# Two edits to a linear attention with two MLPs: where hosted heads make their x, and when the first layer's split weights are stored

## The chip, the core and the metric

The kernel runs on one core of a Trainium2 chip. The metric is device time in microseconds (us) of one execution, lower is better; the kernel before takes 1578.41 us, the median of 3 runs (1578.3 to 1580.91).

## What is computed

Eight batches of eight heads of 576 tokens with 64 columns go through a linear attention with an RMS norm; the heads side by side make 4608 rows of 512 columns, which go through two MLPs (512 to 2048 to 512) in float32.

```
kv  = einsum('bhsd,bhse->bhde', k, v)
out = einsum('bhsd,bhde->bhse', q, kv)
x   = out / sqrt(mean(out*out, -1) + 1e-6) * g_norm        # heads joined: [4608, 512]
h   = x @ w_in
g   = where(h >= 1, h, where(h <= -1, 0, (h + 1)**2 / 4))
x1  = g @ w_out
h2  = x1 @ w_in2
out = relu(h2)**2 @ w_out2
```

The weights arrive as 64-bit numbers; the kernel narrows them itself.

## The kernel before, in words

Every float32 matrix product is made of three TensorE products: both operands are split into a high part and a low rest, and hi x hi, hi x lo and lo x hi are summed in PSUM (`mm3`, L234; in the later phases L858). One such group of three stands in the listings as a row with `x3`.

The columns are taken in blocks of 512 tokens, one block `b` for each batch. **Blocks 0 to 4 of the first MLP are plain** (`PLAIN = 5`). A block has NF = 16 steps `f`. Step `f` computes twelve matmuls into `ph_b_f` (`h_stage`), ACT and DVE make of it `u_b_f` (L682 and L220 on ACT, then L684 on DVE, which frees the PSUM bank of `ph`; two such banks rotate), a split into hi and lo makes `gs_b_f` (L213 on ACT, L226 on DVE), and twelve matmuls add `gs_b_f` times the second weight to four PSUM banks `acc_b` (`out_stage`, two steps later). The first weight `w_0_f` and the second `w_1_f` are loaded as `raw`, narrowed (L264 on ACT, L266 and L267 on DVE as `d`) and split (L182) once, in block 0. All `w_0_f` and `w_1_0` to `w_1_6` stay in SBUF; `w_1_7` to `w_1_15` go to DRAM at once and come back in each later block as tail weights `wt_7` to `wt_15` through three buffers (`load_tail`, L294, SP's queue). Beside that, blocks 1 to 4 prepare the second MLP's weights and sums of both MLPs' weights for the later phases (`prep_...`: raw loads on SP, narrowing L266/L267, sums L334 to L358, splits L182, stores `wsd<-s` issued by ACT, L174).

**The later phases work on pairs of blocks** with seven products in place of eight (`in_phase`, `out_phase`, L858). They read their weights `ws` from the DRAM tiles `wsd`. So the split weights of the first MLP have to be in `wsd` too: `keep_first` stores the parts that the sums don't make, 23 stores (16 of `w_0_f`, 512 KB each for f below 8 and 256 KB above; 7 of `w_1_f`, 256 KB each) on SP's queue. A table of half steps decides when the program writes them: `hook(s, ...)` means step s // 2, first or second half.

**Attention** is done a pair of heads at a time, `hp` = 0 to 3 in a block. `kv_stage` makes k^T v in a PSUM tile `pkv` (L478), ACT copies it into two block-diagonal tiles `kvbd` (L213). `t_stage` transposes q to `qT` on DVE (L548). `o_stage` multiplies (`po`, L557) and ACT makes of each half the square twice (L566 into `s`, L567 into `wk`) and, times the gain, `o` (L205); DVE makes the low rest `s2lo` (L572). `r_stage` sums the squares (`pr`, L586), ACT makes the reciprocal root y (L587) and its square `t` (L220), DVE multiplies o by y (L592), makes a Newton step (`newton`, L516, two halves) and `norm` (L519), the last product that gives x. `pkv`, `po` and `pr` share two PSUM banks (`at`), so each of them waits until the one before the last has been read. The tile `o` is `work[1]`, tag `wk1`, one buffer; `t` in the hosted case is a tile of tag `q`, two buffers that it shares with the loads of q.

The attention of block b is done within block b - 1. That of batches 5 to 7 is **hosted** in the paired phases n = 0 and 1 (`HOSTED`, six pairs of heads each), and there `r_stage` stores x to DRAM (`xpd`, 256 KB, and the last 64 columns `xrd`, 32 KB), on SP's queue.

The order on each engine is static: a scheduler places all instructions by its own estimate of the data's readiness, and the chip then runs each engine's list in order. DMA issues stand in the lists of SP and ACT.

Of the kernel before, what the change touches and what calls it, by code (L numbers as in the profile page):

```python
# [70 lines left out]
def linear_attention_rms_two_mlps(  # L71
# [12 lines left out]
    nc = tc.nc  # L84
# [7 lines left out]
    TB = 512  # L92
# [41 lines left out]
    xpd = {b: dr.tile([P, KD, TB], F32, name=f"xpd{b}") for b in range(PLAIN, B)}  # L134
    x1d = [dr.tile([P, KD, TB], F32, name=f"x1d{b}") for b in range(NB)]
    xrd = dr.tile([P, KD, B, REM], F32, name="xrd")
# [63 lines left out]
    def engine(op, phase):  # L200
        return engines[next(turns[op][min(phase, 2)])]
# [16 lines left out]
    def square(e, dst, src):  # L218
        if e is nc.scalar:
            e.activation(dst, src, AF.Square)  # L220
        else:
            e.tensor_tensor(dst, src, src, ALU.mult)

    def split(t, src, op, phase):
        hi = copy(engine(op + "_hi", phase), t[:, 0, :], src)
        lo = engine(op + "_lo", phase).tensor_tensor(  # L226
            t[:, 1, :], src, t[:, 0, :].bitcast(F32), ALU.subtract
        )
        return hi, lo
# [159 lines left out]
    def bank(b, name):  # L389

        pool, tag = next(banks) if b == 0 else (ps_t, "at")
        return pool.tile([P, TB], F32, tag=tag, name=name)
# [122 lines left out]
    def newton(t, m):  # L515
        nc.vector.scalar_tensor_tensor(t, m, 1e-6, t, op0=ALU.add, op1=ALU.mult)  # L516

    def norm(dst, t, o):
        nc.vector.scalar_tensor_tensor(dst, t, -3.0, o, op0=ALU.add, op1=ALU.mult)  # L519
# [54 lines left out]
    def r_stage(b, hp):  # L574
        (y, o), _ = hl.pop((b, hp))
        if (b, hp) in WHOLE:
            products = [(ones.bitcast(F32), y)]
        else:
            products = [(ones, s2) for s2 in og.pop((b, hp))]
        ms = []  # L580
        for half in range(2):
            c = slice(half * U, (half + 1) * U)
            ps = bank(b, f"pr_{b}_{hp}_{half}")
            m = ps[:, :U]
            for n, (one, s2) in enumerate(products):
                nc.tensor.matmul(m, one, s2[:, c], start=n == 0, stop=n == len(products) - 1)  # L586
            nc.scalar.activation(y[:, c], m, AF.Abs_reciprocal_sqrt, bias=epsb)  # L587
            ms.append((c, m))
        pool, tag = (ap1, "wk2") if b < PLAIN else (ap2, "q")
        t = pool.tile([P, S], F32, tag=tag, name=f"t_{b}_{hp}")  # L590
        square(engine("y", b), t, y)
        nc.vector.tensor_tensor(o, o, y, ALU.mult)  # L592
        for c, m in ms:
            newton(t[:, c], m)
        if b < PLAIN:
            norm(t, t, o)
            nc.gpsimd.tensor_copy(xrem[b][:, hp, :], t[:, TB:])
            split(xs[1, b][hp], t[:, :TB], "x", b)
            return
        norm(o, t, o)  # L600
        nc.sync.dma_start(xpd[b][:, hp, :], o[:, :TB])
        nc.sync.dma_start(xrd[:, hp, b, :], o[:, TB:])

    def new_x(L, b):
        xs[L, b] = [
# [23 lines left out]
    def attention(base, every, order):  # L629

        slots = []
        for j, (b, hp) in enumerate(order):
            s = base + int(every * j)
            turn.setdefault((b, hp), len(turn))
            if b == 1:
                slots += [(max(0, s - 7), load_kv, b, hp), (s, kv_stage, (b, hp))]
            elif j % 2 == 0:
                two = order[j : j + 2]
                turn.setdefault(two[-1], len(turn))
                slots += [(max(0, s - 7), load_kv, *i) for i in two]  # L640
                slots.append((s - (1 if j else 0) - (b < PLAIN and j > 0), kv_stage, *two))
            slots += [
                (max(0, s - (7 if b < PLAIN or j < 2 else 5)), load_q, b, hp),
                (s, t_stage, b, hp),
                (s + 4, o_stage, b, hp, 0),
                (s + 5, o_stage, b, hp, 1),
            ]
            late = 8 if b < PLAIN else 7
            if j == 0 and b < PLAIN:
                slots.append((s + late, begin, b))  # L650
            slots.append((s + late, r_stage, b, hp))
        if b < PLAIN:
            slots.append((2 * NF * b + 2, store_xrem, b))
        return slots
# [426 lines left out]
    def hook(s, f, *a):  # L1081
        hooks.setdefault((s // 2, s % 2), []).append((f, a))
# [17 lines left out]
    last = 2 * (PLAIN - 1) * NF  # L1100
    kept = [(w, f) for f in range(NF) for w in range(2) if w == 0 or f < NF - TAIL]
    for j, (w, f) in enumerate(kept):
        hook(14 + 2 * j, keep_first, w, f)

    units = (
# [201 lines left out]
```

## Time and profile before

| | |
|---|---|
| median of 3 runs | 1578.41 us (1578.3 to 1580.91) |
| profiled execution | 1577.31 us |
| its span in the profile | 1575.5 us |
| granted TensorE clock, mean | 0.993 |
| PE busy | 1544.7 us, 98% of the span |
| DVE, ACT busy | 74%, 57% |
| moved by DMA | 388.14 MB, mean 246 GB/s |

The page gives busy time for each engine, the span in 40 slices and the chain that ended last; 87% of that chain is PE. PE is the engine to watch: a stretch in which it is not busy, or in which the clock granted to it is under 1.00, is lost time. The windows (busy time of each engine in a stretch) show such stretches, the timeline of PE shows in brackets how long it was idle ahead of an instruction and which engine and line released it, and the timelines of DVE, ACT and SP at that time show what stood ahead of the releaser in its queue.

### The profile page before, as it was taken

Reading aid. Unit: us, or ns where it says so; the run is one execution under the profiler, and the core shown is the slowest. Engines: PE = TensorE matmul, PEld = TensorE weight load, DVE = VectorE, ACT = ScalarE, POOL = GpSimd, SP = SyncE. Lnnn points to the kernel's source line nnn. Section 1 sums busy time; section 2 is a strip of 40 time slices with the busy share of each in tenths; the row PEclk is TensorE's granted clock in tenths of the full one; section 3 lists DMA queues with packets and bytes.
Section 4 is the critical chain, followed back from the end, with each engine's and each line's share of the span. In section 5 each row is a group of like instructions: output and inputs, shape, how many; then the busy total and the mean of one; then the engine's idle time right before and its main releaser. Section 6 shows DMA issues by size and latency. Waiting matters only on the chain.

```text
span 1575.5 us, 22117 instructions
## 1 busy us (share of the span) xinstructions
PE 1544.7 (98%) x7581; PEld 1268.8 (81%) x7581; DVE 1169.7 (74%) x2033; ACT 896.1 (57%) x1693; POOL 10.8 (1%) x30
## 2 busy tenths in 40 slices
PE   9999989999999999998999999999999999999999
PEld 5777768887877788787778888888888888888899
DVE  6975777776789668964789788868884597559666
ACT  5875756666656556734566466546653464446354
POOL 0000000000000000000000000000000000000000
PEclk9999999999999999999999999999999999999999
DMA  9776899897799967789867877776776676977797
GB/s 282 199 231 208 239 338 293 278 288 235 237 341 343 334 200 212 243 226 220 250 187 234 229 240 244 223 218 196 245 233 207 198 242 198 243 243 214 223 391 249
DMA packets 330911, 388.14 MB, mean 246 GB/s; under 512 B 197808, under 2 KB 223408, under 8 KB 330800
## 3 DMA queue, kind: packets, MB, share of 16 engines
q1 hardware_dynamic: 299904, 330.63, 70.1%
q10 hardware_dynamic: 30896, 56.11, 9.8%
q8 instruction: 60, 0.98, 0.2%
q14 instruction: 51, 0.42, 0.1%
HBM read 300.42 MB, written 86.25 MB: 245 GB/s over the span
## 4 chain that ended last, share of the span: by engine, by line
PE 87%; DMA 4%; DVE 4%; ACT 3%; issue 1%; SPq 1%; ACTq 0%; DVEq 0%
PE ph L858 31%; PE po L858 31%; PE acc L234 11%; PE ph L234 10%; PE po L557 2%; DMA wt<-wsd 1%; PE pkv L478 1%; PE pr L586 1%; DMA wsd<-s 1%; DVE s L182 1%; DMA ws<-wsd 1%; DMA v<-in_v_dram 0%; DVE u L684 0%; DMA k<-in_k_dram 0%; DVE x L787 0%
## 5 line engine op out<-in xcount | busy, mean ns | idle before, releaser
L858 PE MATMUL ph<-x,ws 128*128 128x512 f32 (+1 forms) x2352 | 508.7, 377 | 0.5 <-DVE u L684 0.5
L858 PEld LDWEIGHTS ph<-x,ws 128*128 128x128 f32 x2352 | 421.0, 190 | 81.0 <-DVE u L684 0.9
L858 PE MATMUL po<-t,ws 128*128 128x512 f32 x2016 | 462.4, 390 | 0.8 <-DVE t L787 0.8
L858 PEld LDWEIGHTS po<-t,ws 128*128 128x128 f32 x2016 | 377.9, 188 | 80.7 <-DVE t L787 2.2
L787 DVE TENSOR_TENSOR t<-g,t 128x512 fp32r<-128x512 f32 (+1 forms) x336 | 216.3, 649 | 86.4 <-ACT t L213 82.9
L213 ACT CAST t<-g 128x512 fp32r<-128x512 f32 (+1 forms) x336 | 195.5, 590 | 117.7 <-PE po L858 63.3
L234 PE MATMUL ph<-x,w 128*128 128x512 f32 x960 | 241.2, 397 | 8.5 <-DVE u L684 7.4
L234 PEld LDWEIGHTS ph<-x,w 128*128 128x128 f32 x960 | 178.4, 188 | 52.3 <-DVE u L684 10.7
L935 ACT ACTIVATE g<-h 128x512 f32<-128x512 f32 (+1 forms) x120 | 70.6, 589 | 111.8 <-DVE h L924 111.8
L234 PE MATMUL acc<-gs,w 128*128 128x512 f32 x528 | 132.4, 395 | 0.4 <-ACT w L213 0.2
L924 DVE CUSTOM_DVE_ANT_0 h<-ph,e 128x512 f32<-128x512 f32 (+1 forms) x120 | 76.3, 637 | 61.0 <-PE ph L858 56.9
L914 DVE TENSOR_TENSOR e<-ph,e 128x512 f32<-128x512 f32 (+1 forms) x112 | 72.3, 650 | 61.3 <-PE ph L858 56.5
L234 PEld LDWEIGHTS acc<-gs,w 128*128 128x128 f32 x528 | 98.2, 188 | 22.2 <-ACT w L213 0.9
L234 PE MATMUL acc<-gs,wt 128*128 128x512 f32 x432 | 107.6, 398 | 3.9 <-DVE gs L226 2.2
L234 PEld LDWEIGHTS acc<-gs,wt 128*128 128x128 f32 x432 | 82.0, 191 | 22.3 <-DVE gs L226 2.6
L213 ACT CAST gs<-u 128x512 fp32r<-128x512 f32 x80 | 49.7, 622 | 65.0 <-DVE u L684 48.8
L682 ACT ACTIVATE u<-ph,halfb 128x512 f32<-128x512 f32 x80 | 55.2, 690 | 48.0 <-PE ph L234 36.1
L213 ACT CAST x<-xr 128x512 fp32r<-128x512 f32 (+1 forms) x98 | 57.2, 589 | 43.1 <-DVE xr L838 24.3
L226 DVE TENSOR_TENSOR gs<-u,gs 128x512 fp32r<-128x512 f32 x80 | 54.9, 687 | 27.0 <-ACT gs L213 26.5
L684 DVE SCALAR_TENSOR_TENSOR u<-u,ph 128x512 f32<-128x512 f32 x80 | 54.3, 681 | 24.1 <-ACT u L220 24.0
L787 DVE TENSOR_TENSOR x<-xr,x 128x512 fp32r<-128x512 f32 (+1 forms) x98 | 63.1, 648 | 2.6 <-ACT x L213 2.6
L911 ACT COPY e<-ph 128x512 f32<-128x512 f32 (+1 forms) x56 | 30.8, 554 | 56.4 <-PE ph L858 49.5
(127 smaller groups left out, 1547.0 us busy)
## 6 DMA issues: line engine op xcount, KB each, us to landing
ws<-wsd SPq DMA_DIRECT2D x392, 512.0 KB, 4.4
wsd<-s ACTq DMA_DIRECT2D x96, 512.0 KB, 5.5
wt<-wsd SPq DMA_DIRECT2D x36, 512.0 KB, 5.5
raw<-in_moe_w_in_dram SPq DMA_DIRECT2D x32, 512.0 KB, 6.6
raw<-in_moe_w_out_dram SPq DMA_DIRECT2D x32, 512.0 KB, 6.5
xr<-x1d SPq DMA_DIRECT2D x36, 256.0 KB, 5.4
out_dram<-ov SPq DMA_DIRECT2D x142, 64.0 KB, 3.5
wsd<-w SPq DMA_DIRECT2D x17, 512.0 KB, 4.2
```

The source lines that it names most:

```text
L213: return e.copy(dst, src)
L226: lo = engine(op + "_lo", phase).tensor_tensor(t[:, 1, :], src, t[:, 0, :].bitcast(F32), ALU.subtract)
L234: nc.tensor.matmul(dst, wt(a), xt(c), start=first and n == 0, stop=last and n == 2)
L557: nc.tensor.matmul(ps[:, :U], kv, qT[:, c], start=True, stop=True)
L682: nc.scalar.activation(u, ps, AF.Relu, bias=halfb, scale=0.5)
L684: nc.vector.scalar_tensor_tensor(u, u, 1.0, ps, op0=ALU.min, op1=ALU.max)
L787: engine2(op + "_lo").tensor_tensor(t[:, 1, :], src, t[:, 0, :].bitcast(F32), ALU.subtract)
L858: nc.tensor.matmul(ps, wt(a), xt(c), start=first and n == 0 and i == 0, stop=last and n == len(lhs) - 1 and i == 2, skip_group_check=True,)
L911: nc.scalar.copy(e[i, 1], bank)
L914: nc.vector.tensor_tensor(e[i, p], bank, e[i, 1], ALU.add)
L924: nc.vector._custom_dve(TENSOR_ADD_SAT, out=h, in0=bank, in1=add, s0=float("inf"), s1=0.0)
L935: nc.scalar.activation(g, h, AF.Square)
```

## The change

```diff
@@ r_stage, for the hosted heads @@
-        norm(o, t, o)
-        nc.sync.dma_start(xpd[b][:, hp, :], o[:, :TB])
-        nc.sync.dma_start(xrd[:, hp, b, :], o[:, TB:])
+        norm(t, t, o)
+        nc.sync.dma_start(xpd[b][:, hp, :], t[:, :TB])
+        nc.sync.dma_start(xrd[:, hp, b, :], t[:, TB:])
@@ the 23 stores of the first layer's split weights @@
     kept = [(w, f) for f in range(NF) for w in range(2) if w == 0 or f < NF - TAIL]
     for j, (w, f) in enumerate(kept):
-        hook(14 + 2 * j, keep_first, w, f)
+        hook(16 + 2 * j // 3, keep_first, w, f)
```

The first edit makes x in the tile `t` in place of `o` and stores it from there. The second moves the 23 stores from half steps 14, 16, ... 58 (one for each step, from step 7 of block 0 to step 13 of block 1) to half steps 16 to 30, that is (2 * j) // 3, three for every two half steps, all within block 0.

No instruction is added or left out; the order changes. The first edit alters it in the paired phase n = 1, the second at the end of block 0 and in block 1. In names, `ph_1_10` is block 1, step 10; in the hosted stage `ph_6_3` is product 6, tile 3, `h_4_3`, `h_3_3` are what DVE makes of the products, and `po_0_0`, `pr_3_1` carry the pair of heads and the half. `pkv_0` and `pkv_2` are made for two pairs at once.

**Place 1: DVE in block 1.** Before, from the split of a prepared second weight (`s_1_0_1`) to `u` of step 10:

```order
L182 TENSOR_TENSOR s_1_0_1_1984<-d_1_8_1914,s_1_0_1_1984 128x2x256
L357 TENSOR_TENSOR s_2_1_0_1953<-s_2_1_0_1953,d_1_0_1884 128x256
L358 TENSOR_TENSOR s_2_1_0_1954<-d_1_8_1914,s_2_1_0_1953 128x256
L334 TENSOR_TENSOR j_0_2011<-w_1_0_490 128x512
L182 TENSOR_TENSOR s_1_0_2_1987<-s_2_1_0_1953,s_1_0_2_1987 128x2x256
L182 TENSOR_TENSOR s_1_0_3_2008<-s_2_1_0_1954,s_1_0_3_2008 128x2x256
L355 TENSOR_TENSOR s_1_1_0_2040<-j_0_2011 128x256
L548 STREAM_TRANSPOSE qT_3_2116<-q_3_1906 128x576
L684 SCALAR_TENSOR_TENSOR u_1_10_2110<-u_1_10_2110,ph_1_10_2097 128x512
```

Now, around the same `u_1_10`:

```order
L684 SCALAR_TENSOR_TENSOR u_1_9_2068<-u_1_9_2068,ph_1_9_2055 128x512
L548 STREAM_TRANSPOSE qT_2_1911<-q_2_1687 128x576
L226 TENSOR_TENSOR x_2_1_1744<-t_1_1950,x_2_1_1744 128x512
L226 TENSOR_TENSOR gs_1_9_2083<-u_1_9_2068,gs_1_9_2083 128x512
L266 TENSOR_SCALAR d_1_0_1891<-raw_1_0_1701 128x512
L684 SCALAR_TENSOR_TENSOR u_1_10_2114<-u_1_10_2114,ph_1_10_2101 128x512
L267 SCALAR_TENSOR_TENSOR d_1_0_1891<-raw_1_0_1701,d_1_0_1891 128x512
```

`u_1_10` has moved ahead of the narrowing, sums and splits of that weight. Some rows above stands `u_1_8`:

```order
L572 TENSOR_TENSOR s2lo_1_1834<-wk_2_1_1671,s_2_1_1805 128x576
L182 TENSOR_TENSOR s_0_0_2_1867<-s_1_0_0_1861,s_0_0_2_1867 128x2x256
L182 TENSOR_TENSOR s_0_0_3_1887<-s_1_0_0_1862,s_0_0_3_1887 128x2x256
L684 SCALAR_TENSOR_TENSOR u_1_8_2009<-u_1_8_2009,ph_1_8_1996 128x512
L592 TENSOR_TENSOR wk_2_1_1672<-wk_2_1_1672,wk_2_1_1671 128x576
L516 SCALAR_TENSOR_TENSOR t_1_1950<-pr_1_0_1942,t_1_1950 128x288
L516 SCALAR_TENSOR_TENSOR t_1_1950<-pr_1_1_1946,t_1_1950 128x288
L226 TENSOR_TENSOR gs_1_8_2021<-u_1_8_2009,gs_1_8_2021 128x512
```

Before, `s2lo_1` and these two splits stood two steps earlier, ahead of `u_1_6`; now `u_1_8` stands behind them.

**Place 2: PE in block 1.** Before, where pair 0 and 1's `pr` and the `pkv` of pairs 2 and 3 stand:

```order
L586 MATMUL pr_1_0_1935<-s_2_1_1796,ones 128x288
L586 MATMUL pr_1_0_1935<-s2lo_1_1826,ones 128x288
L234 MATMUL acc_1_2_1618<-gs_1_5_1806,w_1_5_676 128x512
L234 MATMUL acc_1_3_1619<-gs_1_5_1806,w_1_5_676 128x512 x2
L234 MATMUL ph_1_8_1990<-x_1_0_760,w_0_8_660 128x512 x3
L234 MATMUL ph_1_8_1990<-x_1_1_761,w_0_8_660 128x512 x3
L478 MATMUL pkv_2_1828<-v_3_1673,k_3_1670 64x64 x8
L478 MATMUL pkv_2_1828<-rest_129 64x64 x2
L234 MATMUL ph_1_8_1990<-x_1_2_762,w_0_8_660 128x512 x3
L234 MATMUL ph_1_8_1990<-x_1_3_763,w_0_8_660 128x512 x2
L586 MATMUL pr_1_1_1939<-s_2_1_1796,ones 128x288
L586 MATMUL pr_1_1_1939<-s2lo_1_1826,ones 128x288
```

Now, with `po_1` in the same piece:

```order
L557 MATMUL po_1_0_1803<-qT_1_1673,kvbd_131 128x288
L557 MATMUL po_1_1_1829<-qT_1_1673,kvbd_131 128x288
L234 MATMUL ph_1_9_2055<-x_1_3_763,w_0_9_730 128x512 x2
L478 MATMUL pkv_2_1836<-v_2_1678,k_2_1675 64x64 x8
L478 MATMUL pkv_2_1836<-rest_128 64x64 x2
L586 MATMUL pr_1_0_1942<-s_2_1_1805,ones 128x288
L586 MATMUL pr_1_0_1942<-s2lo_1_1834,ones 128x288
L478 MATMUL pkv_2_1836<-v_3_1684,k_3_1681 64x64 x8
L478 MATMUL pkv_2_1836<-rest_129 64x64 x2
L586 MATMUL pr_1_1_1946<-s_2_1_1805,ones 128x288
L586 MATMUL pr_1_1_1946<-s2lo_1_1834,ones 128x288
L234 MATMUL ph_1_10_2101<-x_1_0_760,w_0_10_786 128x512 x3
```

Between them ph and acc matmuls stood before; now `po_1`, `pkv_2` and `pr_1` stand together, ahead of `ph_1_10`. Further up `ph_1_2` to `ph_1_5` now stand ahead of `pkv_0` and of the first `acc_1` rows. On ACT, `u_1_8`'s L220 stands behind L566, L567 and L205 of both halves of `po_1`, two casts and two stores of a prepared weight, L587 and the `kvbd` copies. On SP the 23 stores are gone from between the loads of block 1; eight more than before stand ahead of its first k load, and `wt_8` still stands behind `raw_1_4` and `raw_1_12`.

**Place 3: PE and DVE in phase n = 1.** PE before, from the last `pr` of pair 3 to the first matmuls behind `po_0`:

```order
L586 MATMUL pr_3_0_7391<-s_6_3_7282,ones 128x288
L586 MATMUL pr_3_0_7391<-s2lo_3_7311,ones 128x288
L586 MATMUL pr_3_1_7395<-s_6_3_7282,ones 128x288
L586 MATMUL pr_3_1_7395<-s2lo_3_7311,ones 128x288
L858 MATMUL ph_5_2_7260<-x_1_3_0_6495,ws_0_1_3_7210 128x512 x3
L858 MATMUL ph_5_2_7260<-x_1_3_1_6697,ws_0_1_3_7210 128x512 x3
L858 MATMUL ph_5_3_7270<-x_1_3_0_6495,ws_0_1_3_7210 128x512 x3
L858 MATMUL ph_5_3_7270<-x_1_3_1_6697,ws_0_1_3_7210 128x512 x3
L557 MATMUL po_0_0_7468<-qT_0_7360,kvbd_130 128x288
L557 MATMUL po_0_1_7496<-qT_0_7360,kvbd_130 128x288
L858 MATMUL ph_1_4_7370<-x_1_1_0_6338,ws_0_2_1_7241 128x512 x3
```

PE now:

```order
L858 MATMUL ph_6_3_7181<-x_1_4_0_6520,ws_0_1_4_7170 128x512 x3
L858 MATMUL ph_6_3_7181<-x_1_4_1_6720,ws_0_1_4_7170 128x512 x3
L557 MATMUL po_0_0_7468<-qT_0_7360,kvbd_130 128x288
L858 MATMUL ph_5_2_7260<-x_1_3_0_6495,ws_0_1_3_7210 128x512 x3
L858 MATMUL ph_5_2_7260<-x_1_3_1_6697,ws_0_1_3_7210 128x512 x3
L858 MATMUL ph_5_3_7270<-x_1_3_0_6495,ws_0_1_3_7210 128x512 x3
L858 MATMUL ph_5_3_7270<-x_1_3_1_6697,ws_0_1_3_7210 128x512 x3
L557 MATMUL po_0_1_7496<-qT_0_7360,kvbd_130 128x288
L586 MATMUL pr_0_0_7557<-s_7_0_7470,ones 128x288
L586 MATMUL pr_0_1_7561<-s_7_0_7470,ones 128x288
L586 MATMUL pr_0_0_7557<-s2lo_0_7501,ones 128x288
L586 MATMUL pr_0_1_7561<-s2lo_0_7501,ones 128x288
```

DVE now, over the same stretch:

```order
L924 ISA h_4_2_7294<-ph_6_2_7172,e_1_1_7152 128x512
L519 SCALAR_TENSOR_TENSOR t_3_7399<-t_3_7399,wk_6_3_7167 128x576
L924 ISA h_4_3_7303<-ph_6_3_7181,e_1_1_7152 128x512
L548 STREAM_TRANSPOSE qT_0_7360<-q_0_7205 128x576
L924 ISA h_3_2_7346<-ph_5_2_7260,e_1_1_7179 128x512
L924 ISA h_3_3_7355<-ph_5_3_7270,e_1_1_7179 128x512
L941 TENSOR_TENSOR t_1_2_7362<-g_1_2_0_7153 128x512
L942 TENSOR_TENSOR g_1_2_0_7153<-g_1_2_1_7154,g_1_2_0_7153 128x512
L941 TENSOR_TENSOR t_1_3_7365<-g_1_3_0_7163 128x512
L572 TENSOR_TENSOR s2lo_0_7501<-wk_7_0_7358,s_7_0_7470 128x576
```

`pkv_0` and `pr_3` have moved 24 matmuls up, `po_0_0` stands directly behind `ph_6_3`, and the four `pr_0`, which stood 60 matmuls behind `po_0_1`, follow it at once. On DVE `qT_0` (L548) stood behind `h_4_3` before too, but on PE the `pkv`, the `pr` and twelve ph matmuls then lay between `ph_6_3` and `po_0_0`. Later in the same phase `pr_1_1` and `po_2_0` stay where they were, and `pkv_2` and `pr_1_0` move 24 matmuls up.

## Rows read from the trace of the kernel before

**Rows 1.** Windows: window, us, busy us of PE, PEld, DVE, ACT, POOL, clock, DMA share, GB/s.

```profile
100.00:120.00 20.00, 19.77 (x105) 15.91 (x104) 14.74 (x26) 14.96 (x31) 0.24 (x1) 1.00 0.55 212
180.00:200.00 20.00, 16.52 (x90) 12.94 (x88) 14.42 (x26) 13.31 (x29) 0.24 (x1) 0.99 0.86 255
200.00:220.00 20.00, 16.12 (x60) 12.78 (x61) 14.36 (x28) 7.96 (x15) 0.24 (x1) 0.83 0.98 338
720.00:740.00 20.00, 17.50 (x71) 14.05 (x70) 9.94 (x16) 9.04 (x18) 0.00 (x0) 0.91 0.88 197
740.00:760.00 20.00, 19.05 (x119) 15.49 (x118) 14.07 (x22) 10.35 (x24) 0.00 (x0) 1.00 0.88 234
780.00:800.00 20.00, 16.06 (x93) 12.63 (x92) 9.86 (x16) 9.57 (x22) 0.00 (x0) 0.83 0.41 139
```

**Rows 2.** Timeline, PE, block 1: start, us, instruction, count, idle before and releaser.

```profile
202.26 0.80 PE L234 MATMUL ph<-x,w 128*128 128x512 f32 x1 [5.73 <-DVE u L684]
...
210.27 5.75 PE L234 MATMUL acc<-gs,wt 128*128 128x512 f32 x24 [1.62 <-DMA wt<-wsd]
```

**Rows 3.** Timeline, DVE, block 1.

```profile
198.84 1.29 DVE L182 TENSOR_TENSOR s<-s,s 128x512 fp32r<-128x512 f32 x2
...
201.51 0.69 DVE L684 SCALAR_TENSOR_TENSOR u<-u,ph 128x512 f32<-128x512 f32 x1 [0.23 <-ACT u L220]
```

**Rows 4.** Timeline, ACT, block 1 (ACTq: its DMA issues).

```profile
197.90 0.62 ACT L213 CAST s<-s 128x512 fp32r<-128x512 f32 x1 [1.15 <-DVE s L357]
...
199.56 0.97 ACTq L174 DMA_DIRECT2D wsd<-s  x2
200.85 0.63 ACT L220 ACTIVATE u<-u 128x512 f32<-128x512 f32 x1 [1.82 <-DVE s L355]
```

**Rows 5.** Timeline, SP's queue, end of block 0 and block 1.

```profile
144.27 4.41 SPq L159 DMA_DIRECT2D wsd<-w  x4
...
201.30 0.94 SPq L294 DMA_DIRECT2D wt<-wsd  x1
```

**Rows 6.** Timeline, PE, hosted attention.

```profile
724.75 1.66 PE L557 MATMUL po<-qT,kvbd 128*128 128x288 f32 x4 [2.50 <-DVE t L516]
...
746.58 0.69 PE L478 MATMUL pkv<-kv 128*64 128x64 f32 x16
...
749.37 0.40 PE L586 MATMUL pr<-s,ones 128*128 128x288 f32 x1 [0.95 <-ACT kvbd L213]
...
787.86 0.40 PE L586 MATMUL pr<-s,ones 128*128 128x288 f32 x1 [0.90 <-ACT kvbd L213]
...
791.43 1.33 PE L557 MATMUL po<-qT,kvbd 128*128 128x288 f32 x2 [3.04 <-DVE qT L548]
```

**Rows 7.** Timeline, DVE, hosted attention.

```profile
749.20 0.77 DVE L548 STREAM_TRANSPOSE qT<-q 128x576 f32<-128x576 f32 x1
...
751.20 0.82 DVE L516 SCALAR_TENSOR_TENSOR t<-pr,t 128x288 f32<-128x288 f32 x2
...
754.11 0.69 DVE L941 TENSOR_TENSOR t<-g 128x512 f32<-128x512 f32 x1
...
756.05 0.75 DVE L572 TENSOR_TENSOR s2lo<-wk,s 128x576 fp32r<-128x576 f32 x1
```

**Rows 8.** Timeline, ACT, hosted attention.

```profile
717.31 0.50 ACT L205 ACTIVATE wk<-po,gvec 128x288 f32<-128x288 f32 x1
...
718.27 0.53 ACT L205 ACTIVATE wk<-po,gvec 128x288 f32<-128x288 f32 x1
...
748.47 0.86 ACT L213 COPY kvbd<-pkv 64x64 f32<-64x64 f32 x4
749.35 1.10 ACT L587 ACTIVATE wk<-pr,epsb 128x288 f32<-128x288 f32 x2
...
758.29 0.89 ACT L205 ACTIVATE wk<-po,gvec 128x288 f32<-128x288 f32 x2 [1.26 <-DMA xrd<-wk]
```

**Rows 9.** The page's DMA issues: operation, count, KB each, us to landing.

```profile
xpd<-wk SPq DMA_DIRECT2D x12, 256.0 KB, 3.1
```

## The prediction, made before the changed kernel was run

> **What bounds the kernel now.** I read the windows of 20 us first, then the engines' timelines around the poor ones, then the DMA queue. TensorE is what the time is made of: in a sound window it is busy for all of its 20 us at granted clock 1.00, and time is lost only where PE idles or its clock falls. The windows name two such places that the change touches. In block 1 (180 to 220 us) PE is busy for 16.52 and 16.12 of 20 us, and the clock of the second window is 0.83 [rows 1]. In the hosted attention (720 to 800 us) it is busy for 17.50, 19.05 and 16.06 us, at 0.91, 1.00 and 0.83 [rows 1]. A clock that averages 0.83 over 20 us costs up to 0.17 x 20 = 3.4 us, and 0.91 up to 1.8.
>
> Block 1 first. PE waits 5.73 us for the DVE instruction u and 1.62 us for the tail weight wt [rows 2]. That u (L684, step 10) starts on DVE at 201.51, only after two splits of a weight preparation [rows 3], and its ScalarE half (L220, 200.85) stands behind two stores that ACT issues [rows 4]: a queue's order, not work, makes PE wait. The wt transfer was issued at 201.30, when PE had already stopped [rows 5]. Loss there: 5.73 + 1.62 = 7.35 idle, and 0.2 + 3.4 of clock from the two windows: **11.0 us**. In the hosted stage I read four waits: 2.50, 0.95, 0.90 and 3.04 us [rows 6], each for a copy or a DVE step of a head.
>
> **Edit 1 (x over t).** No instruction is added or removed; the store's source changes, so the tile that the store holds is t and not o. What this frees is the next head's L205, which writes o. In the trace just one of the twelve heads waited there, 1.26 us on ACT [rows 8], and PE did not wait for it: worth 0. What it burdens is the next t. Two t or q buffers rotate, a head comes about every 19 us (the pr of one head is at 749.37, that of the next but one at 787.86 [rows 6]), and a store lands 3.1 us after its issue [rows 9]: no wait, 0, with some 15 us of cover. A store that landed three times as late would still be covered. So the direct effect is nothing, and what counts is the order that the scheduler now writes in phase n=1. By the listing in the section on the change:
> - pr_3_1 waits for the four kvbd copies, as now (0.95 [rows 6]); ACT now has L587 and a cast ahead of them, so **+0.4**.
> - po_0_0 stands directly behind the last matmul of ph_6_3, and its qT stands on DVE behind h_4_3, which needs that same matmul. One 128x512 step 0.69 and the transpose 0.77 [rows 7]: **+1.5**, where there was no wait.
> - pr_0 now follows po_0_1 at once. Its s2lo comes on DVE behind h_3_3, L941, L942 and L941, four steps of 0.69 and its own 0.75 [rows 7], 3.5 us from the end of ph_5_3, less some 0.8 that PE has to do: **+2.7**. Before, 60 matmuls lay between.
> - pr_1_1 is 24 matmuls later, which covers the kvbd copies: -0.90. po_2_0 behind it then waits for the chain L587, L592, two L516, L519, transpose: 0.55 + 0.76 + 0.82 + 0.76 + 0.77 = 3.7 [rows 7, 8] (the 128x576 steps at 0.76) in place of 3.04: +0.6. Together **-0.3**.
> Sum +4.3. The clock: five and a half us of idle fall into some 16 us from 742. A lone 0.95 in a window left it at 1.00, 2.50 took it to 0.91, 3.94 to 0.83 [rows 1, 6]. These waits are each under 3, so I take the middle one, **+1.8** (ends 0 and 3.4). Edit 1: **+6.1**, 4.3 to 7.7.
>
> **Edit 2 (the 23 stores).** The same 23 stores of 512 or 256 KB (7.8 MB; 17 of them, 5.5 MB, stood behind block 1's first loads) now leave SP within or just after block 0. There the DMA engines have room: 0.55 busy at 100 to 120 us [rows 1]. SP has eight more stores ahead of block 1's first k. Four took it 4.41 us [rows 5], so k is issued some 9 us later; but PE needs k some 11 us later than before, since the four times twelve matmuls of ph_1_2 to ph_1_5 (2.7 us each) now come ahead of pkv_0. So 0. If a store took SP twice as long, 18 less 11 = 7 us would show, which is the upper bound; PE did not wait for SP's loads there, so no gain is to be had.
> In block 1 the 5.73 goes: u_1_10 now stands ahead of the preparation that it was behind. What is late next is a clump. po_1, pkv_2 and pr_1, which were spread between ph and acc matmuls, now stand in a row between ph_1_9 and ph_1_10, and ph_1_10 needs the bank that u_1_8 frees. u_1_8's L220 stands on ACT behind: two sets of L566, L567, L205 at 0.96 a set (from one L205 to the next [rows 8]), two casts of 0.62, L587 at 0.55, two store issues 0.97, the kvbd copies 0.87; with itself 0.63 and L684 0.69 on DVE that is 6.9 us [rows 3, 4, 8]. PE has 1.84 for two pkv halves and two pr (746.58 to 749.37 without the wait), 0.40 for two more pr [rows 6] and 0.45 for two matmuls: 2.7. Wait **4.2**. ph_1_11 then needs u_1_9, behind L587, L682 and L220 on ACT and L516, gs, L519 on DVE, about 4.2 us against the 2.7 of twelve matmuls: **1.5**. wt_8 stands on SP behind raw_1_4 and raw_1_12, whose buffers are freed only after u_1_10; with about 5 us from issue to use, PE waits 0 to 3.5, and I take **1.7**. The clock lies between 1.00 and the 0.83 of today's 7.35 idle: 0 to 3.4, **1.7**. New loss 9.1 against 11.0: **-1.9**, from -9.5 (only the first 1.5 of it comes) to +3.
>
> **Sum.** The profiled execution took 1577.31; +6.1 - 1.9 = +4.2 gives 1581.5. The median of the runs lies 1.1 above that execution; I go half of it up, to **1582**, own range 1578.5 to 1586. The bound of no change, 0.2%, is 3.2 us, so 1575.2 to 1581.6.
>
> A rule that would alter the clock terms is in the Trainium skill, "TensorE: Matmul & The Clock Gate", section "A second HAM failure mode: psum-queue depth-cycling": a kernel whose PE paused briefly and often between groups, as it went round its PSUM banks, had its clock swing between the two levels. The lone 0.95 at full clock [rows 1, 6] does not show this, but no window here has five such waits together. By that rule both clumps would run at 1.2 GHz for a time, which is the third rival, at 1587; without it the clock terms would be 0 and the sum 3.5 lower, at 1578.
>
> **Rivals.**
> 1. *Faster.* Block 1 gives nearly all back. Place: u_1_10 and u_1_8 on DVE and ACT. If the casts and store issues ahead of u_1_8 are done before po_1 arrives (their inputs do not depend on po_1), PE waits little and the clock stays: 1.5 lost in place of 11.0, -9.5. With hosted waits of 4.3 at full clock: 1577.3 - 5.2 = 1572, some 1573 by the median. It decides from 7.5 us given back. For it: 5.5 MB leave a stretch where the DMA engines were 0.86 to 0.98 busy [rows 1]. Against: the kvbd copies do depend on the clump.
> 2. *No change.* Block 1 gives back 5 (wt_8 in time, clock full) and the hosted stage takes 6.1: 1578.4, by the median 1579.5.
> 3. *Slower still.* Both clumps at the lower clock and wt_8 at its worst: hosted 1.6 more (7.7), block 1 1.7 of clock and 1.8 of wt_8 more, so 1581.5 + 1.6 + 3.5 = 1586.6, by the median 1587. For it: 0.83 in both places already today.
> 4. *The order costs nothing.* The listing holds no times: if PE comes to po_0_0 and pr_0 later than I count, it finds their inputs made, and block 1's clump only takes the place of the 7.35 us of today. Then the changed kernel does what it says and stays at 1578. Against: both hosted inputs depend on the very matmul ahead of the wait.
>
> **How the numbers follow.** Forecast 0.41, rivals 0.22, 0.20, 0.12, 0.05. The forecast's low end lies within 0.2% (0.08 of its 0.41). Faster 0.22; within 0.2%: 0.20 + 0.05 + 0.08 = 0.33; slower 0.33 + 0.12 = 0.45. The range 1572 to 1587 leaves out about half of the first rival and some of the third.
>
> **What would show it.** Right: in the changed profile po_0_0 waits 1.5 for qT and pr_0 2.5 to 3 for s2lo and L205, in the window from 740; the 5.73 for u is gone and shorter waits for kvbd, u and wt stand after po_1, at about 185 to 210. Wrong: windows 180 to 220 at 19 or more of 20, or the hosted windows no worse than now. A wait of L220's t for a store of xpd would make the first edit's 0 wrong; a PE wait for v or k at 145 to 155, the second's.

## The result, and the profile after

The changed kernel takes **1595.01 us**, median of 4 runs (1592.14 to 1596.37), against 1579.66 (1578.30 to 1582.27): ratio **1.0093, 95% interval 1.0072 to 1.0114**, 15 us slower. I had forecast slower, 1582, and a range to 1587; the time lies outside it. The head of the profile's page, of an execution that took 1595.61 us:

```profile
span 1593.7 us, 22135 instructions
PE 1554.4 (98%) x7581; PEld 1271.6 (80%) x7581; DVE 1169.7 (73%) x2033; ACT 897.4 (56%) x1693; POOL 10.7 (1%) x30
```

The span is 18.2 us longer than before: PE is idle for 8.5 of these (39.3 in place of 30.8) and busy for 9.7 more at the same 7581 matmuls. The mean granted clock went from 0.993 to 0.990, which stands for some 4.8 of the 9.7. Both executions can also be timed from one matmul to the same matmul. The changed one is 2.0 us later at its first `ph`. The 400 `ph` and `acc` matmuls that begin with block 1's first take it 6.8 us longer (121.0 against 114.2). The hosted stage takes it 5.2 longer (from the `ph` behind its first `pkv` to the first product of `out_phase`: 717.69 to 818.48, against 707.22 to 802.86), and what follows directly 1.4 longer. The other 2.8 lie in stretches that differ by as much from one kernel of this document to another. The medians lie 15.3 apart, so some 3 us of the 18 belong to the two executions and not to the change.

The windows of the changed kernel, the two stretches of [rows 1] (busy us of PE, PEld, DVE, ACT, POOL, then clock, DMA share, GB/s; the hosted stage now begins some 10 us later):

```profile
180.00:200.00 20.00, 16.02 (x93) 12.02 (x92) 14.76 (x28) 10.59 (x25) 0.24 (x1) 0.87 0.89 277
200.00:220.00 20.00, 14.41 (x54) 10.28 (x53) 14.74 (x29) 13.42 (x27) 0.24 (x1) 0.84 0.81 255
220.00:240.00 20.00, 20.00 (x86) 16.48 (x85) 14.51 (x30) 7.05 (x15) 0.00 (x0) 0.94 0.92 291
240.00:260.00 20.00, 18.62 (x114) 14.68 (x114) 17.93 (x33) 14.93 (x30) 0.64 (x1) 1.00 1.04 322
720.00:740.00 20.00, 15.69 (x68) 12.24 (x67) 9.53 (x15) 10.45 (x23) 0.00 (x0) 1.00 0.91 230
740.00:760.00 20.00, 18.06 (x113) 14.39 (x111) 11.26 (x18) 8.87 (x18) 0.00 (x0) 1.00 0.98 231
760.00:780.00 20.00, 16.70 (x65) 13.27 (x66) 10.11 (x17) 9.09 (x18) 0.00 (x0) 0.91 0.58 158
800.00:820.00 20.00, 16.36 (x61) 13.05 (x60) 9.12 (x14) 7.56 (x14) 0.00 (x0) 0.83 0.50 127
```

Block 1 has lost 3.98 + 5.59 + 1.38 us of idle and, at 0.87, 0.84 and 0.94, some 7 us of clock: 18 us in place of 11. The hosted stage, which was the sure part of the forecast, is next. PE's timeline there:

```profile
728.34 0.40 PE L586 MATMUL pr<-s,ones 128*128 128x288 f32 x1 [1.22 <-ACT wk L205]
729.34 0.40 PE L586 MATMUL pr<-s,ones 128*128 128x288 f32 x1 [0.60 <-ACT wk L205]
...
735.27 1.24 PE L557 MATMUL po<-qT,kvbd 128*128 128x288 f32 x4 [2.50 <-DVE t L516]
...
753.49 0.40 PE L586 MATMUL pr<-s,ones 128*128 128x288 f32 x1 [1.40 <-ACT kvbd L213]
...
760.94 0.75 PE L557 MATMUL po<-qT,kvbd 128*128 128x288 f32 x2 [1.47 <-DVE qT L548]
...
766.64 0.40 PE L586 MATMUL pr<-s,ones 128*128 128x288 f32 x1 [1.58 <-ACT wk L205]
767.82 0.53 PE L586 MATMUL pr<-s2lo,ones 128*128 128x288 f32 x2 [0.79 <-DVE s2lo L572]
...
806.99 1.33 PE L557 MATMUL po<-qT,kvbd 128*128 128x288 f32 x2 [3.64 <-DVE qT L548]
```

The first three waits are those of before (the 2.50 is in [rows 6]; the other two, from the kernel before):

```profile
717.87 0.40 PE L586 MATMUL pr<-s,ones 128*128 128x288 f32 x1 [1.23 <-ACT wk L205]
718.86 0.40 PE L586 MATMUL pr<-s,ones 128*128 128x288 f32 x1 [0.59 <-ACT wk L205]
```

Then come the four that the order was read for: 1.40 for kvbd, 1.47 for qT, 1.58 + 0.79 for pr_0, 3.64 for qT. All eight make 13.2 us; the six of before made 9.2. The clock took no more than before: one window at 0.91 and one at 0.83 in both kernels. In block 1:

```profile
154.39 0.69 PE L478 MATMUL pkv<-v,k 128*64 128x64 f32 x16
...
187.27 1.24 PE L557 MATMUL po<-qT,kvbd 128*128 128x288 f32 x4
...
189.27 0.69 PE L478 MATMUL pkv<-v,k 128*64 128x64 f32 x16 [0.30 <-ACT wk L205]
...
190.26 0.40 PE L586 MATMUL pr<-s,ones 128*128 128x288 f32 x1 [0.19 <-ACT wk L205]
...
192.75 0.69 PE L478 MATMUL pkv<-v,k 128*64 128x64 f32 x16 [1.69 <-DMA v<-in_v_dram]
...
194.50 0.40 PE L586 MATMUL pr<-s,ones 128*128 128x288 f32 x1 [0.95 <-ACT kvbd L213]
...
195.88 6.42 PE L234 MATMUL ph<-x,w 128*128 128x512 f32 x15 [0.85 <-DVE u L684]
...
214.90 0.87 PE L557 MATMUL po<-qT,kvbd 128*128 128x288 f32 x2 [2.05 <-DVE t L516]
218.47 10.23 PE L234 MATMUL acc<-gs,wt 128*128 128x512 f32 x36 [2.71 <-DMA wt<-wsd]
...
241.83 3.47 PE L234 MATMUL ph<-x,w 128*128 128x512 f32 x14 [1.18 <-DVE u L684]
```

The 5.73 of [rows 2] is gone, and eleven smaller waits have come. The clump after po_1 (187.27) waits 0.30, 0.19, 1.69, 0.95 and 0.85. After it 15 matmuls take 6.42 us, nearly twice their time, and then follow 2.05 for the bank of po_3, 2.71 for wt and 1.18 for u, with smaller ones between. pkv_0 stands at 154.39 with no wait ahead of it, though SP had issued its k long before:

```profile
120.07 14.73 SPq L159 DMA_DIRECT2D wsd<-w  x12
134.85 1.20 SPq L418 DMA_DIRECT2D k<-in_k_dram  x1
...
157.65 7.93 SPq L159 DMA_DIRECT2D wsd<-w  x10
...
183.24 0.39 SPq L421 DMA_DIRECT2D v<-in_v_dram  x1
```

k goes out at 134.85, after twelve stores in 14.73 us. In the kernel before it went out only 3.35 us earlier:

```profile
131.50 0.84 SPq L418 DMA_DIRECT2D k<-in_k_dram  x1
```

So pkv_0 is late because PE's list has it late. SP's waits from 155 to 192 us (what was waited for, total us, how many, longest) show two that no listing of names tells (the kernel before has such waits too, 7.5 us for `wsd<-s` ahead of a k, 4.6 for x1d):

```profile
SPq L159 <- DMA x1d<-ev: 14.3, 2, 13.4
SPq L421 <- DMA wsd<-s: 7.5, 1, 7.5
```

The ten stores behind the first loads stood 13.4 us for a transfer that ACT issues (x1d, the result of block 0), and the v of pair 2 stood 7.5 us for one of ACT's `wsd<-s`.

### The profile page after: what moved, and what is told of

It reads as the page before. It is cut to its first block, busy times and chain, and to the rows that moved or that the text cites. A ratio compares the mean times of both kernels' runs of the same rounds, so it can differ in the third digit from the quotient of the medians.

```text
span 1593.7 us, 22135 instructions
## 1 busy us (share of the span) xinstructions
PE 1554.4 (98%) x7581; PEld 1271.6 (80%) x7581; DVE 1169.7 (73%) x2033; ACT 897.4 (56%) x1693; POOL 10.7 (1%) x30
## 4 chain that ended last, share of the span: by engine, by line
PE 85%; DMA 7%; DVE 5%; ACT 2%; issue 1%; SPq 0%; ACTq 0%; DVEq 0%
PE ph L858 31%; PE po L858 30%; PE acc L234 10%; PE ph L234 9%; DMA wsd<-s 2%; DMA wt<-wsd 2%; DMA v<-in_v_dram 1%; PE po L557 1%; PE pkv L478 1%; PE pr L586 1%; DMA ws<-wsd 1%; PE pwarm L1161 0%; DVE t L787 0%; DVE s L182 0%; DMA k<-in_k_dram 0%
## 5 line engine op out<-in xcount | busy, mean ns | idle before, releaser
L787 DVE TENSOR_TENSOR t<-g,t 128x512 fp32r<-128x512 f32 (+1 forms) x336 | 217.1, 652 | 87.6 <-ACT t L213 80.0
L226 DVE TENSOR_TENSOR gs<-u,gs 128x512 fp32r<-128x512 f32 x80 | 55.1, 688 | 24.6 <-ACT gs L213 24.0
L787 DVE TENSOR_TENSOR x<-xr,x 128x512 fp32r<-128x512 f32 (+1 forms) x98 | 63.6, 654 | 2.0 <-ACT x L213 2.0
```

The source lines that it names most:

```text
L226: lo = engine(op + "_lo", phase).tensor_tensor(t[:, 1, :], src, t[:, 0, :].bitcast(F32), ALU.subtract)
L787: engine2(op + "_lo").tensor_tensor(t[:, 1, :], src, t[:, 0, :].bitcast(F32), ALU.subtract)
```

## The experiments

All ratios are against the kernel before, run on the same chip: 1578.9 to 1580.4 in the four sets.

**e1, e2: one edit each.** The first edit alone (`norm(t, t, o)` and the stores from t), and the second alone (`hook(16 + 2 * j // 3, ...)`).

> The first edit alone (x made over t, stores where they were before). My theory: the loss of the hosted stage comes from this edit and is a matter of order: po_0_0 waits 1.5 us for qT, pr_0 some 2.4 for L205 and s2lo, po_2_0 3.6 for qT, with the clock lower once; blocks 0 and 1 as before. Time 5 to 6.5 us over the kernel before, about 1585.5. Rival: the first edit is free and the whole loss comes from the stores in block 1, which shifted the hosted stage against its loads: then 1579.7 here, within 1.5 us.

Measured 1587.79, ratio 1.0049 (1.0031 to 1.0066), +4.9 to +10.4 us. The windows 180 to 220 of this run are as before (16.91 and 15.85 busy, clock 1.00 and 0.83), and its hosted stage has the eight waits of the changed kernel, each within 0.02 us, and takes the same 5.2 us longer. The price is above the 5 to 6.5 us that I had expected.

> The second edit alone (stores in block 0 on SP's queue, x made over o). My theory: block 1 loses 18 us in place of 11, the hosted stage is as before: 7 to 9 us over the kernel before, about 1587.5. Rival (the first edit makes all of it): 1579.7.

Measured 1584.91, ratio 1.0036 (1.0027 to 1.0046), +5.7 us, under my 7 to 9. Its waits in block 1 are those of the changed kernel, within 0.6 us each. The two are separate terms: 0.49% and 0.36% make 0.85% of the 0.93%. Both rivals fall.

**e2 on ACT: the same stores at the same half steps, another queue.** `e` is a new argument of `keep_halves`; `keep_first` passes `nc.scalar`.

```diff
-            nc.sync.dma_start(dst, t[:, hs])
+            e.dma_start(dst, t[:, hs])
```

> The second edit alone, with the 23 stores issued by ACT's queue at the same half steps; the same bytes in block 0. Queue theory: what hurts is that 13 stores stand on SP ahead of block 1's k, v and q, so that its attention comes late and in a clump; with SP free block 1's pkv, po and pr stand apart, the 1.69 for v and the waits of the clump go, and block 1 loses 2 to 6 us in place of 18: 1571 to 1576. Traffic theory: the bytes in block 0 collide with the loads whoever issues them: 1586 to 1589. Third: ACT is held by its store issues and u comes late: block 0 loses some us in the place of block 1, 1580 or more.

Measured 1562.84, ratio **0.9889 (0.9873 to 0.9905)**, 17.5 us faster than the kernel before by the ratio, and under my 1571 to 1576. Its windows of block 1, and the first of the hosted stage:

```profile
180.00:200.00 20.00, 20.00 (x90) 16.49 (x90) 17.42 (x33) 13.38 (x27) 3.65 (x1) 1.00 0.88 281
200.00:220.00 20.00, 20.00 (x91) 16.50 (x90) 15.99 (x31) 13.13 (x27) 0.24 (x1) 1.00 1.05 319
700.00:720.00 20.00, 15.69 (x68) 12.28 (x68) 11.97 (x18) 9.50 (x21) 0.00 (x0) 1.00 0.94 237
```

Block 1 loses nothing, with the DMA engines at 0.88 and 1.05, where the changed kernel had 0.89 and 0.81. So bytes in this stretch are not the cause: the traffic theory falls.

**e3: the stores in blocks 2 and 3, on SP.** `hook(64 + 2 * j, ...)`.

> The 23 stores at half steps 64, 66 to 108 (blocks 2 and 3, one for each step, on SP), x made over o. Queue theory: block 1 is rid of them as in the ACT case and loses 2 to 6 us in place of the 11 of the kernel before; blocks 2 and 3 have loads at any half step to stand behind, but no first k that everything waits for, and lose at most 3: 1571 to 1577. Traffic theory: the DMA engines are 0.9 to 1.09 busy in block 2, the stores collide there and the loss of block 1 comes back in blocks 2 and 3: 1580 or more.

Measured 1567.00, ratio 0.9914 (0.9896 to 0.9933), under my 1571 to 1577. Block 1 and the stretch where the stores now stand are all at 20.00 busy, clock 1.00.

**e9: stores on ACT, at the old half steps** (`14 + 2 * j`).

> The kernel before with only the queue changed: 23 stores on ACT at the old half steps 14, 16 to 58. The order of PE in block 1 is the same as with the early stores on ACT. If SP's queue is all that matters and the half steps do not: 1561 to 1565, as with the early stores on ACT. If early storing on ACT gained because ACT has time in block 0 and not in block 1: 3 to 8 us more, 1566 to 1571, with PE waiting for u in block 1.

Measured 1564.31, ratio 0.9897 (0.9882 to 0.9911). Early or late makes no difference on ACT. At both sets of half steps the queue made it: with the same stores on SP the times were 1579.58 (old half steps, the kernel before) and 1584.91 (early, e2). Of PE in block 1, this kernel, e2 on ACT and e3 have the same order: pkv_0 after 24 matmuls, po_0 after 70, pr_0 after 108, and all pairs apart. (The kernel before, counting block 1's matmuls alone: 57, 103, 108; the changed kernel: 98, 144, 147.)

**e11, e12: which part of the 23, and is it order or queue?** Two things were still mixed: the order on PE, which the scheduler wrote, and SP's queue on the chip, which holds loads behind stores. The first + line is e11, the second e12; the stores that are left go to blocks 2 and 3.

```diff
-        hook(14 + 2 * j, keep_first, w, f)
+        hook((16 + 2 * j // 3 if j >= 14 else 64 + 2 * j), keep_first, w, f)
+        hook((16 + 2 * j // 3 if j < 14 else 64 + 2 * j), keep_first, w, f)
```

> The second edit for the last nine of the 23 stores alone: with w_1_15 they are the ten that stand on SP behind block 1's first k, v, q and ahead of raw_0, q_1, k_2 and v_2, as in the changed kernel; the other 14 go to block 2 and later (half steps 64 + 2 j). The order of PE in block 1 is nearly that of the stores on ACT: pkv_0 after 24 matmuls, po_0 after 70, pr_0 after 108. Order theory: block 1 loses 0 to 4 us, as there; 1565 to 1571. Queue theory (SP, held by these ten, brings q_1, k_2, v_2 too late): block 1 loses 8 us or more, with PE waiting for v or qT; 1578 to 1585.

Measured 1566.66, ratio 0.9928 (0.9907 to 0.9948), as the order theory had it.

> The other part: the first 14 stores where the second edit puts them, on SP ahead of block 1's first k; the last nine in block 2 and later. Nothing but w_1_15 stands on SP behind that k and q. The order of PE in block 1 is that of the changed kernel up to pr_0 (pkv_0 after 98 matmuls, po_0 after 144) and then tight: po_1, pkv_2 and pr_1 between 191 and 198. Order theory: the loss of block 1 stays, 10 us or more: 1576 to 1585. Queue theory: gone with the ten: 1565 to 1571.

Measured 1575.16, ratio 0.9973 (0.9960 to 0.9985). The windows of e11 and then of e12:

```profile
180.00:200.00 20.00, 19.84 (x88) 16.10 (x88) 19.33 (x39) 15.07 (x29) 0.37 (x1) 1.00 0.96 324
200.00:220.00 20.00, 20.00 (x90) 16.49 (x89) 14.16 (x28) 10.64 (x21) 0.24 (x1) 1.00 1.08 335
```

```profile
180.00:200.00 20.00, 16.25 (x95) 12.57 (x96) 17.46 (x32) 16.87 (x37) 0.64 (x1) 0.92 0.92 261
200.00:220.00 20.00, 20.00 (x90) 16.49 (x89) 16.55 (x33) 13.56 (x28) 0.24 (x1) 1.00 1.01 349
```

In e11 the ten stores stand on SP where they do in the changed kernel, take 11.17 us to issue (5.4 of it waiting for x1d), and PE loses 0.16 us: with a good order the queue alone costs nothing that block 1 shows. In e12 the clump is back with hardly a store behind the loads, and PE loses 5.1 us of idle (1.38 of it just ahead of 180) and 1.6 of clock. None of its waits there is for a load; the three longest:

```profile
180.22 0.69 PE L478 MATMUL pkv<-v,k 128*64 128x64 f32 x16 [1.53 <-ACT wk L205]
...
184.14 1.66 PE L234 MATMUL ph<-x,w 128*128 128x512 f32 x6 [1.40 <-DVE u L684]
...
196.21 4.61 PE L234 MATMUL ph<-x,w 128*128 128x512 f32 x12 [1.61 <-DVE u L684]
```

So the order alone costs. The 400 matmuls of block 1 say the same: 102.9 us in e11, 110.5 in e12, and 102.1 to 102.2 in e3, e9 and e2 on ACT. But e12 is 8.5 us over e11, just under what I had expected, and 4.5 us under the kernel before, whose 400 take 114.2, although its attention comes later (98 matmuls against 57). So it is not lateness by itself that costs, but what stands together in the order.

Both parts together (e2, 1584.91) are some 10 over e12, and its 400 matmuls take 121.4. In e2, 4.4 us of PE's idle in block 1 are waits for loads (1.59 for v, 2.79 for wt), which e12 does not have. The ten cost nothing where the attention is early and make it worse where it is late already; how this second part divides between order and queue was not separated. SP's long wait for x1d is not enough for it: one store in e12 stood 13.1 us there.

**e8: the loads ahead of the stores.** The second edit, with the k, v and q loads of block 1's first two pairs ten half steps earlier (`s - 17` in place of `s - 7`). This load overwrites the last rows of k and v (`rest`) before block 0's last pair has used them, so that pair's kv is of other rows; the work is the same.

> The second edit alone (23 stores on SP in block 0), but the k, v and q loads of block 1's first two pairs ten half steps earlier, so that they stand on SP ahead of the stores. Bytes, queue and half steps of the stores are those of the second edit. Its order has pkv_0 after 22 and po_0 after 70 of block 1's matmuls, as with the stores on ACT, in place of 98 and 144; pairs 1 to 3 still come late (pkv_2 after 194, with po_2 and pr_2 in one clump at 238). Order theory: block 1 loses less than the 18 us of the second edit alone: some 8 to 12; 1575 to 1580. Rival (transfers of the stores themselves slow block 1): 1584 to 1586, as the second edit alone.

Measured 1586.86, ratio 1.0048 (1.0030 to 1.0066), no gain over e2 and outside both expectations. The end of block 0 and the one poor window of block 1:

```profile
120.00:140.00 20.00, 11.85 (x38) 7.82 (x37) 12.77 (x22) 11.44 (x24) 0.61 (x2) 0.59 0.28 86
200.00:220.00 20.00, 16.01 (x60) 12.57 (x59) 17.77 (x35) 13.00 (x27) 0.64 (x1) 0.83 1.07 360
```

Block 1 did lose less, 4.0 idle and 3.4 of clock in place of 18. But 8.15 us and a clock of 0.59 were lost at 120 to 140, where nothing had been lost before. They are five waits of one clump of `pr`, `po` and `pkv` at the end of block 0 (123 to 134 us). The total says nothing for either theory; the loss moved to another place in the order.

**e4, e5, e10, e6, e7: the hosted stage.** One line puts `r_stage` of all hosted heads a half step later:

```diff
-            late = 8 if b < PLAIN else 7
+            late = 8
```

e4 is the kernel before with this line, and e5 has the first edit too. e6 is both edits with the stores on ACT, at the old `late`; e7 is the stores on ACT with the later `r_stage`, without the first edit; e10 is e6 with `late = 8`, so both edits and both remedies.

> The kernel before with the hosted heads' r_stage one half step later (8 in place of 7); neither edit. The order of phase n=1 then has pr, pkv and po apart, with 12 or more matmuls between nearly all of them; only po_1 with pr_1 at the phase's start stay together. Order theory: of the 14 us that the hosted stage loses (9.2 idle, 5.2 clock) the 2.50, 0.95, 0.90 and 3.04 go, and the clock with them: 8 to 12 us under the kernel before, 1567 to 1571. Rival: DVE and ACT lack the time there and the waits move to t L787 and u: within 2 us of 1579.

Measured 1572.66, ratio 0.9950 (0.9935 to 0.9965).

```profile
720.00:740.00 20.00, 19.90 (x81) 16.19 (x82) 9.60 (x16) 7.67 (x14) 0.00 (x0) 0.91 0.93 221
740.00:760.00 20.00, 19.41 (x119) 15.48 (x118) 13.85 (x23) 11.25 (x25) 0.00 (x0) 1.00 0.79 210
780.00:800.00 20.00, 19.73 (x122) 15.95 (x121) 15.11 (x25) 12.90 (x29) 0.00 (x0) 1.00 0.67 195
```

2.50, 0.95, 0.90 and 3.04 are gone: 0.10, 0.59 and 0.27 us are left of the 2.50, 0.95 and 3.94 in these windows. The gain is some 7.8 us, just under the 8 to 12 that I had expected, and one part of the rival came true: 2.07 us of new waits for t (L787) stand behind the stage, at 833 and 836.

> The first edit with the same later r_stage. If the first edit costs only by the order that it brings about, its price over the kernel with the later step alone is that of three tight places in this order (pkv_0 and pr_3_0 at once behind po_3_1; pkv_2 and pr_1 behind po_1_1; pr_3_0 behind po_3_1): each needs a bank that L205 frees, 1 to 1.5 us, in all 2 to 5: 1571 to 1575. If storing from t has a price of its own (next t waits for the store), it is 7 to 9 over that kernel, and L220 shows a wait for a DMA.

Measured 1570.90, ratio 0.9937 (0.9922 to 0.9952). The first edit costs nothing here: 1.8 us less than e4, with intervals that overlap. That is under my 1571 to 1575, so the three places that I called tight cost nothing that can be seen. ACT's L220 waits for no store of xpd or xrd in this run, nor in the changed kernel.

> Both edits, the 23 stores on ACT's queue. If the two edits are separate terms, this is the kernel with the stores on ACT (1562.8) plus the first edit alone (1587.8 less 1578.9, some 8): 1570 to 1572. If they act on one another (the hosted stage depends on when its loads were queued), under 1566 or over 1575.

Measured 1571.64, ratio 0.9947 (0.9930 to 0.9964): by the ratios 9.2 over the stores on ACT alone, as the first edit alone is 7.7 over the kernel before. The two are separate terms.

> Stores early on ACT, x over o, hosted r_stage one half step later: the two gains together. If separate: 1562.8 less the 8 to 12 of the later step: 1551 to 1555. If the later step only gains where block 1 is late: 1560 to 1563.

Measured **1555.85, ratio 0.9846 (0.9823 to 0.9868)**: both gains, 24.6 us under the kernel before, and just above my 1551 to 1555.

> Both edits, with the stores on ACT and the hosted r_stage one half step later. If the price of each edit is that of the order alone and both are mended: as without the first edit, 1553 to 1558. If storing from t costs anything by itself: 1562 or more.

Measured **1556.60, ratio 0.9847 (0.9832 to 0.9863)**. This is the change itself, with ACT for the stores and the later `r_stage`:

```profile
180.00:200.00 20.00, 20.00 (x91) 16.51 (x90) 17.45 (x33) 13.47 (x27) 3.65 (x1) 1.00 0.87 279
200.00:220.00 20.00, 20.00 (x91) 16.51 (x90) 15.96 (x31) 12.99 (x27) 0.24 (x1) 1.00 1.08 325
740.00:760.00 20.00, 20.00 (x89) 16.46 (x88) 12.19 (x20) 10.01 (x20) 0.00 (x0) 1.00 1.10 298
760.00:780.00 20.00, 19.55 (x122) 15.86 (x121) 16.06 (x27) 12.49 (x29) 0.00 (x0) 1.00 0.71 195
```

So both edits are in the kernel and neither costs anything, once the stores are off SP's queue and `r_stage` is later: with and without the first edit it is 1556.60 and 1555.85, and on ACT's queue the early and the old half steps made 1562.84 and 1564.31.

## Why the prediction was wrong

**The hosted stage was right, wait by wait, but not in its clock.** The waits: forecast 1.35 for kvbd, measured 1.40; 1.5 for po_0_0, 1.47; 2.7 for pr_0, 2.37; 3.7 for po_2_0, 3.64. Idle rose by 4.0 us where the sum said 4.3. With the clock I had 6.1 (4.3 to 7.7), and the edit alone measured 7.7 by its ratio (4.9 to 10.4). That this is so near is in part luck. The 1.8 for the clock did not come: the windows give it 5.2 us before and 5.2 now, in the changed kernel and in e1. In its place the stage took 1.2 us more than its idle explains, and 1.4 came behind it (0.80 of that a wait for t, L787), which the sum did not have. Why the waits came out: for po_0_0 and pr_0 the instruction that PE waits for stood right behind a step that itself needs PE's last matmul, so no lateness of PE could cover it. The zero for the store from t was right as well (e5).

**The step that failed is the sum for block 1: "New loss 9.1 against 11.0: -1.9".** It lost 18.0 by the windows, +7.0, its 400 matmuls took 6.8 longer, and e2 alone measured +5.7. Part by part:
- The clump of po_1, pkv_2 and pr_1: forecast 4.2, measured 3.98. Right in size, in part by luck: I had one wait at ph_1_10 for u_1_8, and that was 0.85. The banks and kvbd made 1.44 ahead of it, and 1.69 was for v, a load that the sum did not have.
- ph_1_11 waiting for u_1_9: forecast 1.5, measured nothing; the matmuls of ph_1_10 came at the lower clock, 12 of them in some 5.1 us, and that covered the 4.2.
- wt_8: forecast 1.7 of 0 to 3.5, measured 2.71 (and that behind po_3's wait). SP issued it late (213.09) for another reason than the one I gave: the two raw loads were out by 207.2, and it then stood 5.9 us for one of ACT's `wsd<-s`.
- Not in my sum at all: 2.05 for po_3, 0.83 for pr_2, 1.18 for a later u and 0.20 for a later wt, 4.3 us together. I had stopped at the clump. A pair that is late pushes the next pair into less room, and the order of pairs 2 and 3 was in the listing for me to price.
- The clock: forecast 1.7, measured 7.0 against 3.6 before. This is the largest miss. My bound of 3.4 was that of one window, and the lower clock went on over three.

My range took block 1 from -9.5 to +3; 6.8 in place of -1.9 alone puts the sum of 1581.5 at 1590, outside the range.

**The term of the moved stores was 0, and it is 0 for the first k, but I read the order's answer to them as cover.** k went out only some 3 us later than before (134.85 against 131.50 on SP's queue), not 9, and PE never waited for it. The v of pair 2, behind ten of these stores, it did wait for (1.69). I wrote that PE needed k some 11 us later, "since the four times twelve matmuls of ph_1_2 to ph_1_5 (2.7 us each) now come ahead of pkv_0", as if that were help. It was the harm: e11 (pkv_0 after 24 matmuls, 0.16 us lost) against e12 (after 98, 6.7 lost) shows that block 1 pays for the order that came with it. The listing said so: pkv_0 had moved down, though nothing on the chip made it wait.

**Rivals.** The faster one put 0.22 on block 1 giving nearly all back. It does so with the stores on ACT or in blocks 2 and 3, not in this order. The second needed block 1 to give back 5, and the fourth an order at no cost; neither came. The third came nearest (both clumps at the lower clock, 1587). It was too low by 8 us, for the waits behind block 1's clump and the clock's loss over three windows, and its 1.6 more of clock in the hosted stage did not come. The rule of the Trainium skill beside it ("TensorE: Matmul & The Clock Gate", "A second HAM failure mode: psum-queue depth-cycling") agrees with block 1, where many small waits go with 0.87, 0.84 and 0.94. It does not with the changed kernel's 720 to 740, where 4.31 us of idle in three waits left the clock at 1.00.

## What to carry to other kernels

Where a scheduler writes a static order, price a change by what it does to the order, and look for the instruction that moved although nothing on the chip makes it late: there what stands on a queue has gone into the order of the busiest engine (that it goes by way of the scheduler's estimate was not looked at). Stores on the queue that the critical loads share (SP here) cost time where they stood ahead of block 1's first loads (e12), next to nothing where only ten stood behind these loads (e11), and nothing in block 1 when they came in blocks 2 and 3 (e3); a queue of another engine took the same 23 stores at no cost in block 1. When a clump is priced, follow it to the end of the stage: here its waits delayed the next piece, and the clock's loss came on top in three windows.

## What was not expected of the hardware

The same three waits of the hosted stage (1.22, 0.60 and 2.50, idle 4.31 in one window) had the clock at 1.00 in the changed kernel and in the stores on ACT (above) and in e9, at 0.91 in the second edit alone, e3 and e6, and at 0.83 in e8 and e11. The second edit alone and e8:

```profile
720.00:740.00 20.00, 15.70 (x61) 12.16 (x61) 10.99 (x18) 9.26 (x21) 0.00 (x0) 0.91 0.95 245
```

```profile
720.00:740.00 20.00, 15.69 (x54) 11.86 (x54) 9.48 (x14) 7.55 (x18) 0.00 (x0) 0.83 0.91 229
```

So 0, some 1.8 and some 3.4 us go with the same three waits. It is why I can't give the clock's terms better than to some us, and why the sums above are checked by the comparisons and not by one profile.

SP's issues also waited for transfers that ACT had issued (13.4 and 7.5 us in the changed kernel, 5.4 in e11, 7.5 and 4.6 before), though the two queues share no tile there that I can name. Why they do was not tried.
